# Weight pieces gated by the transfer four ahead of them instead of three, and the order planned anew with priorities varied unit by unit

## The chip, the cores and the metric

The kernel runs on one core of a Trainium2 chip. The metric is the device time of one execution in microseconds (us); less is better. The core's engines are TensorE (PE: matmuls, and PEld: its weight loads), VectorE (DVE), ScalarE (ACT), GpSimd (POOL) and SyncE (SP). SP computes nothing here: it issues most of the DMA transfers. Each engine works through its own instructions in the order in which the program emits them; an instruction waits for the semaphores of what it needs.

## The reference

Two stages in one kernel. First a gated linear attention over 4 x 8 heads, 768 positions and a head width of 48, then a two-layer MLP with an exact GELU over all 3072 tokens (model width 384, inner width 2048). All inputs are float32.

```python
f = 1 / (1 + exp(-f_logit))                       # [B, H, S, D] = 4, 8, 768, 48
for t in range(S):
    state = f[:, :, t, :, None] * state + einsum('bhd,bhe->bhde', k[:, :, t], v[:, :, t])
    y[:, :, t] = einsum('bhd,bhde->bhe', q[:, :, t], state)
x = y.transpose(0, 2, 1, 3).reshape(B * S, H * D)  # 3072 x 384
h = x @ w_in                                       # 3072 x 2048
g = 0.5 * h * (1 + erf(h / sqrt(2)))
out = g @ w_out                                    # 3072 x 384
```

## The kernel before

The attention is computed chunk by chunk: 24 chunks of 128 positions, six to a batch row. Two neighbouring chunks make a unit `u` (0 to 11), and the two chunks of a unit make one MLP group `g`. The state passes from chunk to chunk within a batch row and begins anew after six.

For a unit, four transfers bring `fl` (the logits), `kt`, `qt` and `vt`. `decays` has ScalarE compute an exponential and a logarithm (`E`, `L`, lines 466 and 469), TensorE the cumulative sum over the chunk (`C`, lines 482 to 492), ScalarE its exponentials both ways (`RG`, `GT`, lines 497 and 499), VectorE the scaled keys and queries in bf16 (`KP`, `QP`, line 512; two of them on POOL, by `GKP` and `GQP`), and POOL the bf16 copy `vb` of v (`VC`, line 517). `turn` transposes the scaled keys and queries: for the units in `KDMA` a DMA transpose on SP's queue (`KD`, line 533), else PE transposes into PSUM (`Tk`, `Tq`, line 545) and a copy out of it (`KQ`, line 551) by VectorE, or by ScalarE for the chunks in `HKQ`. The scores follow (`A`, lines 649 and 711), their mask on VectorE (line 558), the state (`S`, lines 672 and 733, with `carry` at lines 578 to 589) and the output `Y` (lines 626, 632, 685, 753). Units 0 to 4 (`PAIRS`) take two chunks at once, the rest one after the other.

`outputs` casts Y to bf16 (`YB`, line 602) and turns it for the MLP: for units in `XDMA` one DMA transpose on SP's queue (`XD`, line 606), else three PE transposes per chunk (`XT`, line 618) and a copy by VectorE (`X`, line 621). `ffn_group` then does F1 (line 789: eight steps of six matmuls over 256 tokens), the GELU on ScalarE (line 799), F2 (line 808: for each chunk four steps `r` of four matmuls, step `r` with weight piece `wout[r]`), the copy out of PSUM (lines 815 and 822) and the store on SP (line 824).

The MLP weights come in pieces, cast to bf16 by the transfer: w_in as `win[0]` (1024 columns) and `win[1]`, `win[2]` (512 each), w_out as `wout[0]` to `wout[3]`. POOL issues these (lines 433 and 436).

What sets the order of the work is a planner written into the kernel (`Plan`). Each step is an `Op` with an engine, an assumed duration, what it reads and writes, the buffers it takes, and a priority: 20 per unit for the attention, 1000 more for the MLP matmuls, so that these fill what attention leaves. `run` places the operations one after another on model clocks; among the ones that could start soonest the smaller priority goes first. Then the instructions are emitted in the order of their model starts. A random number within ±`SPREAD`, from the generator with `SEED`, is added to each priority, so that another seed gives another order. The model's numbers go into nothing but the order (and into the amount of filler: up to model time 30, gaps before PE steps are filled with matmuls of `junk`, line 847, whose results nobody reads).

The loads have a list of their own, `LOADS`, that fixes their order. A letter and a number name a piece: `f`, `k`, `q`, `v` the four inputs of a unit, `u` all four, `i` a piece of w_in, `o` a piece of w_out. A piece whose predecessor in the list was issued by the other engine waits for an earlier transfer (`gate`) to have landed:

```python
        if i and order[i - 1][0] != eng:
            back = 3 if eng == "pool" else 2
            for j in range(i - back, -1, -1):
                if order[j][0] != eng:
                    gate = order[j][1]
                    break
```

It looks back from the piece `back` places ahead of it for the nearest transfer of the other engine. By the list of before, i0 waits for v1, i1 for f2, o0 for nothing of its own (its predecessor is also POOL's), and q3 for o2. A wait holds up all that is behind it on the issuing engine: on SP later loads, stores and DMA transposes, on POOL its arithmetic.

Of the kernel before, what the change touches and what calls it, by code (L numbers as in the profile page):

```python
# [22 lines left out]

TURN = 0.1

SPREAD, SEED = (1.0, 78)

EAGER = 0.0

# [5 lines left out]
class Slots:  # L35


    def __init__(self, n, tiles=None):
        self.n, self.tiles = n, tiles
        self.who = [None] * n  # L40

    def new(self):
        return Buf(self)

    def free(self):

        out = []
        for i, b in enumerate(self.who):
            t = 0.0
            if b is not None:  # L50
                for u in b.users:
                    if u.end is None:
                        t = None
                        break
                    t = max(t, u.vis)
            if t is not None:
                out.append((t, i))
        return sorted(out)


class Buf:
# [14 lines left out]
class Plan:  # L76
# [30 lines left out]
    def run(self):  # L107
        free = dict.fromkeys(list(LAT), 0.7)
        free["DMA"] = 1.8
        rng = random.Random(SEED)  # L110
        for o in self.ops:
            if o.prio > -5:
                o.prio += rng.uniform(-SPREAD, SPREAD)
        act, switched, mode = None, 0.0, 0
        port = {"DVE": (0.0, 0.0), "POOL": (0.0, 0.0)}
        for o in self.ops:
            o.outs = []
        for o in self.ops:
            o.left = len(o.deps)
            for d in o.deps:  # L120
                d.outs.append(o)
        ready = [o for o in self.ops if not o.left]
        placed = []
        while ready:
            best = None
            for o in ready:
                t = free[o.eng]
                for d in o.deps:
                    v = d.end if d.eng == o.eng and (o.eng != "DMA" or d is o.chain) else d.vis + o.lag
                    t = v if v > t else t  # L130
                ok, taken = True, {}
                for b in o.bufs:
                    if b.slot is None:
                        v, k = b.slots.free(), taken.get(id(b.slots), 0)
                        if len(v) <= k:
                            ok = False
                            break
                        t = max(t, v[k][0])
                        taken[id(b.slots)] = k + 1
                if not ok:  # L140
                    continue
                x = t
                if o.table and act and o.table != act:
                    x = max(t, min(t + 2 * TABLE, max([d.vis for d in o.deps] + [switched]) + PATIENCE))
                pr = o.prio + (HOLD if o.held and act == "gelu" else 0.0)
                key = (int((x - (EAGER if o.eng == "PE" and o.prio < 900 else 0.0)) * 20 + 0.999), pr, o.seq)
                if best is None or key < best[0]:
                    best = (key, t, o)
            if best is None:
                raise RuntimeError("no operation can be placed: %s" % [o.name for o in ready[:20]])  # L150
            _, t, o = best
            d = o.dur
            if o.eng == "PE" and o.mode != mode:
                mode = o.mode
                d += TURN
            if o.port:
                other = port["POOL" if o.eng == "DVE" else "DVE"]
                d += SHARED * max(0.0, min(other[1], t + d) - max(other[0], t))
            if o.table and o.table != act:
                act, switched = o.table, t  # L160
                d += TABLE
            o.start, o.end = t, t + d
            o.vis = o.end + o.lat
            free[o.eng] = o.end
            for b in o.bufs:
                if b.slot is None:
                    b.slot = b.slots.free()[0][1]
                    b.slots.who[b.slot] = b
            ready.remove(o)
            placed.append(o)  # L170
            if o.port:
                port[o.eng] = (t, o.end)
            for n in o.outs:
                n.left -= 1
                if not n.left:
                    ready.append(n)
        if len(placed) != len(self.ops):
            raise RuntimeError("operations that wait for each other")
        placed.sort(key=lambda o: (o.start, o.seq))
        self.placed = placed  # L180
        return placed
# [14 lines left out]
WIN = [1024, 512, 512]  # L196
# [3 lines left out]
EA = []  # L200
SPLIT = []
HVC = []
HKQ = [0]
HYB = [1]
HX = []
GKP, GQP = ([2], [3])
GAM = []
ODVE = [0, 1, 2, 3, 4, 5, 6, 7, 8, 9, 10, 11, 12, 13, 14, 15, 16, 17, 18, 19, 20, 21, 22, 23]
XDMA = [3, 4, 5, 6, 7, 8, 9, 10, 11]
KDMA = [5, 6, 7, 8, 9, 10, 11]  # L210
AJ = [2, 3, 4, 5, 6, 7, 8, 9, 10, 11]
NGT = 4
WARM = 30.0
LOADS = ['f0', 'q0', 'k0', 'f1', 'v0', 'v1', 'k1', 'q1', 'i0', 'k2', 'f2', 'v2', 'q2', 'i1', 'i2', 'o0', 'o1', 'o2', 'o3', 'q3', 'f3', 'k3', 'v3', 'u4']
LOADS += [f"u{n}" for n in range(12) if f"u{n}" not in LOADS and f"c{2 * n}" not in LOADS and f"f{n}" not in LOADS]


@with_exitstack
def kernel(
# [134 lines left out]
    def load(eng, issue, wr, bufs, dur, name):  # L354
        i = len(order)
        gate = None
        if i and order[i - 1][0] != eng:
            back = 3 if eng == "pool" else 2
            for j in range(i - back, -1, -1):
                if order[j][0] != eng:  # L360
                    gate = order[j][1]
                    break
# [13 lines left out]
        if eng == "pool":  # L376
            if pools:
                gd.append(pools[-1])
            if i > 2 and order[i - 3][0] == "pool":
                gd.append(order[i - 3][1])  # L380
            k = P.add("POOL", 0.8, None, deps=gd, prio=-1000 + i, name="i" + name, lat=1.0)
            o = P.add("DMA", dur, lambda: None, wr=wr, bufs=bufs, prio=i, name=name, chain=prev, deps=[k])
            k.fn = lambda o=o: fn(o)
            pools.append(k)
        else:
            o = P.add("DMA", dur, None, wr=wr, bufs=bufs, prio=i, name=name, chain=prev, deps=gd)
            o.fn = lambda o=o: fn(o)
        if 7 <= i < 30 and o.lat < 1.8:
            o.lat = 1.8
        order.append((eng, o))  # L390

    def src(a, n):
# [9 lines left out]
    for what in LOADS:  # L402
        m = int(what[1:])
        if what[0] in "ucfkqv":
# [19 lines left out]
            else:  # L424
                for j in js:
                    for nm, a in names:
                        if what[0] not in ("u", "c", nm[0]):
# [1 line left out]
                        load("sp", lambda x=x, nm=nm, a=a, m=m, j=j: nc.sync.dma_start(  # L429
                            out=half(m, x[nm], j), in_=src(a, 2 * m + j)),  # L430
                            [(nm, 2 * m + j)], [x[nm]], 1.05, f"{nm}{m}.{j}")
        elif what[0] == "i":
            load("pool", lambda m=m: nc.gpsimd.dma_start(out=win[m], in_=win_src[:, :, wcol[m]:wcol[m] + WIN[m]]),
                 [f"win{m}"], [], {512: 1.97, 1024: 3.95}[WIN[m]] + (0.5 if order[-1][0] == "sp" else 0.0), what)
        elif what[0] == "o":
            load("pool", lambda m=m: nc.gpsimd.dma_start(out=wout[m], in_=wo_src[m]), [f"wout{m}"], [], 2.15, what)
# [450 lines left out]
```

## Time and profile before

| | |
|---|---|
| median of 4 runs | 185.45 us (184.78 to 187.68) |
| the profiled execution | 187.68 us, span 185.7 us, clock 0.991 |
| busy: PE, PEld, ACT, DVE, POOL | 173.9, 133.2, 121.4, 100.4, 53.2 us |
| F1 and F2 matmuls (lines 789, 808) | 69.1 and 67.6 us busy |
| filler matmuls (line 847) | 9.1 us busy |
| moved by DMA | 32.48 MB, 175 GB/s in the mean |

The span runs from the first to the last instruction; the execution's own time has some 2 us around it. In a line of the profile, the engine and the source line stand first, then the operation and its operands; "x18" is how many, and the bracket at the end is how long the engine sat idle before and what ended that. In tables by stretch, the columns are the length of the stretch, then busy time and number of instructions of PE, PEld, DVE, ACT, POOL, then the granted TensorE clock, the busy share of the DMA engines and GB/s. Waits are given as total, times and the longest, in us.

### The profile page before, as it was taken

What the parts mean: (1) busy time and instruction counts of PE and PEld (TensorE: products, weight loads), DVE (VectorE), ACT (ScalarE), POOL (GpSimd) and SP (SyncE); (2) the same over time, 40 slices, a digit from 0 to 9 for tenths busy, and PEclk for the clock granted to TensorE, in tenths of its full rate; (3) what the DMA queues carried; (4) which work ended last, traced back from release to release, by engine and by line L of the source; (5) the groups of instructions that cost most, each with busy time, mean ns of one, the idle gap of its engine ahead of it and who ended that gap; (6) DMA issues with size and microseconds to landing.
All of it is one profiled execution on the core that took longest, in us unless ns stands there. A gap on an engine that the chain in (4) does not pass through costs nothing.

```text
span 185.7 us, 4914 instructions
## 1 busy us (share of the span) xinstructions
PE 173.9 (94%) x1988; PEld 133.2 (72%) x1988; DVE 100.4 (54%) x190; ACT 121.4 (65%) x206; POOL 53.2 (29%) x118
## 2 busy tenths in 40 slices
PE   7897999999999969979999999999899999999992
PEld 2355779866787548967669976588689966797960
DVE  4377940079995898816374411696862717450120
ACT  2781198945769768968365799697589685272700
POOL 7359890005076231122124101424035114000000
PEclk9997899999999999999999999999999999999999
DMA  6999989999999799979899999599999933602112
GB/s 151 261 261 230 266 132 197 204 220 265 247 221 228 149 202 174 214 148 189 137 231 259 185 186 227 95 219 220 145 211 192 179 82 75 184 9 37 42 44 83
DMA packets 106421, 32.48 MB, mean 175 GB/s; under 512 B 101536, under 2 KB 105504, under 8 KB 106400
## 3 DMA queue, kind: packets, MB, share of 16 engines
q1 hardware_dynamic: 104480, 28.94, 75.2%
q0 software_dynamic: 1776, 3.15, 9.6%
q8 instruction: 15, 0.25, 0.6%
q10 hardware_dynamic: 144, 0.10, 0.2%
q14 instruction: 6, 0.05, 0.1%
HBM read 25.17 MB, written 4.72 MB: 161 GB/s over the span
## 4 chain that ended last, share of the span: by engine, by line
PE 68%; DMA 13%; DVE 5%; SPq 5%; ACT 4%; POOL 3%; issue 2%; DVEq 0%; POOLq 0%; ACTq 0%
PE ps L808 28%; PE ps L789 28%; DMA vt<-in_v_dram 8%; DMA xT<-yb 3%; SPq L421 3%; DVE sc L512 2%; DMA fl<-in_f_logit_dram 2%; PE ps L545 2%; PE ps L649 1%; SPq L429 1%; PE ps L482 1%; PE ps L685 1%; DVE kq L551 1%; POOL vb L517 1%; PE ps L672 1%
## 5 line engine op out<-in xcount | busy, mean ns | idle before, releaser
L799 ACT ACTIVATE gT<-ps 128x512 bf16<-128x512 f32 x96 | 58.0, 670 | 22.8 <-PE ps L789 21.5
L789 PE MATMUL ps<-xT,win 128*128 128x256 bf16 x576 | 69.1, 273 | 0.6 <-DMA xT<-yb 0.6
L808 PE MATMUL ps<-wout,gT 128*128 128x384 bf16 x384 | 67.6, 326 | 0.3 <-ACT gT L799 0.3
L789 PEld LDWEIGHTS <-win 128*128 128x128 bf16 x576 | 61.0, 114 | 2.2 <-issue 0.6
L808 PEld LDWEIGHTS <-gT 128*128 128x128 bf16 x384 | 36.2, 98 | 21.6 <-ACT gT L799 0.4
L822 DVE COPY osb<-ps 128x384 f32<-128x384 f32 x23 | 12.8, 555 | 30.8 <-PE ps L808 29.2
L517 POOL CAST vb<-vt 128x384 bf16<-128x384 f32 x24 | 12.1, 516 | 51.0 <-DMA vt<-in_v_dram 51.0
L512 DVE TENSOR_TENSOR sc<-kt,rg 128x384 bf16<-128x384 f32 x23 | 14.0, 613 | 22.1 <-ACT rg L497 17.1
L584 POOL TENSOR_TENSOR tn<-rr,gl 128x384 f32<-128x384 f32 x16 | 14.2, 889 | 34.1 <-DVE rr L582 28.4
L558 DVE TENSOR_TENSOR am<-ps,mask 128x512 bf16<-128x512 f32 x28 | 17.4, 684 | 12.0 <-PE ps L649 11.4
L589 POOL CAST sb<-tn 48x192 bf16<-48x192 f32 x40 | 15.2, 381 | 17.0 <-DVE tn L578 8.6
L853 ACT ACT_TABLE_LOAD x15 | 19.2, 1283 | 0.3
L497 ACT ACTIVATE rg<-ps 128x384 f32<-128x384 f32 x24 | 11.9, 499 | 11.4 <-PE ps L484 5.8
L466 ACT ACTIVATE fl<-fl 128x768 f32<-128x768 f32 x12 | 10.2, 847 | 13.5 <-DMA fl<-in_f_logit_dram 13.3
L512 DVE TENSOR_TENSOR sc<-qt,gt 128x384 bf16<-128x384 f32 x23 | 15.1, 667 | 0.9 <-ACT gt L499 0.9
L602 DVE CAST yb<-ps 128x384 bf16<-128x384 f32 x23 | 12.4, 554 | 4.5 <-PE ps L685 3.0
L499 ACT ACTIVATE gt<-ps 128x384 f32<-128x384 f32 x24 | 11.7, 500 | 3.3 <-PE ps L484 3.3
L558 DVE TENSOR_TENSOR am<-ps,maskp 128x512 bf16<-128x512 f32 x20 | 12.4, 683 | 1.7 <-PE ps L711 1.6
L582 DVE TENSOR_TENSOR rr<-ps,tn 128x384 f32<-128x384 f32 x16 | 8.8, 551 | 5.8 <-PE ps L672 3.0
L847 PE MATMUL ps<-junk 128*128 128x512 bf16 (+2 forms) x28 | 9.1, 464 | 1.4 <-POOL junk L839 1.3
L469 ACT ACTIVATE lf<-fl 128x768 bf16<-128x768 f32 x12 | 10.1, 843 | 0.4
L545 PE MATMUL ps<-ident,sc 128*128 128x128 bf16 x80 | 7.6, 234 | 2.1 <-DVE sc L512 1.1
(65 smaller groups left out, 120.1 us busy)
## 6 DMA issues: line engine op xcount, KB each, us to landing
out_dram<-osb SPq DMA_DIRECT2D x23, 192.0 KB, 2.4
fl<-in_f_logit_dram SPq DMA_DIRECT2D x14, 192.0 KB, 4.2
kt<-in_k_dram SPq DMA_DIRECT2D x14, 192.0 KB, 3.8
qt<-in_q_dram SPq DMA_DIRECT2D x14, 192.0 KB, 3.6
vt<-in_v_dram SPq DMA_DIRECT2D x14, 192.0 KB, 3.8
fl<-in_f_logit_dram SPq DMA_DIRECT2D x5, 384.0 KB, 6.0
qt<-in_q_dram SPq DMA_DIRECT2D x5, 384.0 KB, 4.8
kt<-in_k_dram SPq DMA_DIRECT2D x5, 384.0 KB, 6.2
```

Source lines behind the costliest of these rows:

```text
L497: P.add("ACT", 0.40, lambda g=gps[j], rg=rg: nc.scalar.activation(rg.t(), g.t()[:, 0:HD], AF.Exp, scale=-1.0), rd=[("g", n)], wr=[("rg", n ...
L512: P.add("POOL" if pl else "DVE", 0.80 if pl else 0.475, lambda w=w, a=a, b=b, y=y, j=j, pl=pl: (nc.gpsimd if pl else nc.vector).tensor_tensor(
L517: P.add("ACT" if hv else "POOL", 0.40 if hv else 0.47, lambda y=y, j=j, hv=hv: (nc.scalar.copy if hv else nc.gpsimd.tensor_copy)(y["vb"].t ...
L558: P.add("POOL" if pl else "DVE", 1.15 if pl else 0.61, lambda hh=hh, pl=pl: (nc.gpsimd if pl else nc.vector).tensor_tensor(ams[hh].t(), ap ...
L584: P.add("POOL", 0.83, lambda: nc.gpsimd.tensor_tensor(tn.t(), rr.t(), glb(), ALU.mult), rd=[("rr", n), ("gl", n)], wr=[("tn", n)], bufs=[r ...
L589: P.add("POOL", 0.36, lambda hh=hh: nc.gpsimd.tensor_copy(sb.t()[64 * hh:64 * hh + D, :, D * hh:D * hh + D], tn.t()[64 * hh:64 * hh + D, : ...
L602: P.add("ACT" if help_ else "DVE", 0.40 if help_ else 0.475, lambda: copier(help_)(yb.t()[:, i, :], yp.t()[:, 0:HD]), rd=[("yp", n)], wr=[ ...
L789: nc.tensor.matmul(hps.t()[:, i * tok:(i + 1) * tok].rearrange("a (s t) -> a s t", s=s), col(fo)[:, kk, :], xT.t()[:, :, kk, :], start=(kk ...
L799: nc.scalar.activation(to, fr, AF.Gelu)
L808: nc.tensor.matmul(op.t()[:, 0:d_model], gT.t()[:, fo, s_ * C:(s_ + 1) * C], wout[fo // 4][:, fo % 4, :], start=(fo == 0), stop=(fo == FO ...
L822: P.add("DVE" if od else "ACT", 0.475 if od else 0.40, lambda op=op, osb=osb, od=od: copier(not od)(osb.t(), op.t()[:, 0:d_model]), rd=[(" ...
L853: nc.scalar.preload_act_table_set({"exp": "natural_log_exp_and_others", "gelu": "gelu_and_others"}[o.table])
```

## The change

- A weight piece is gated by the nearest transfer of the other engine at least four places ahead of it, instead of three. SP's gates stay at two.
- `LOADS`: v0 moves ahead of q0 and f1, k0 ahead of q0; o3 goes ahead of o2 and f3 between them; k3 stands ahead of q3. With the new list i0 waits for f1 (now fifth), i1 for k2, f3 for o1, o2 for q2, k3 for o3. The name `i3` in the list issues nothing, since there are three pieces.
- `XDMA` loses units 3 and 4: their output is turned by PE and copied by VectorE.
- `HKQ` gains chunk 2: ScalarE copies its transposed keys and queries instead of VectorE.
- The seed is another, and each unit may add a random number of its own: `SEEDS` has one entry per unit, and its rest after division by four chooses the width.
- The model has three other numbers (the delay of POOL's issue and of gated loads on SP, the landing of i0), and free slots are remembered within the planner. No instruction comes from these lines but through the order.

```diff
-SPREAD, SEED = (1.0, 78)
+SPREAD, SEED = (1.0, 97)
+
+SEEDS = [0, 3, 358, 3531, 1454, 1223, 983, 3849, 2582, 1403, 2107, 2867]
...
         rng = random.Random(SEED)
+        own = [random.Random(x) for x in SEEDS]
         for o in self.ops:
             if o.prio > -5:
+                k = min(max(int(o.prio % 1000) // 20, 0), len(SEEDS) - 1)
                 o.prio += rng.uniform(-SPREAD, SPREAD)
+                if SEEDS[k]:
+                    w = (0.5, 1.0, 3.0, 8.0)[SEEDS[k] % 4]
+                    o.prio += own[k].uniform(-w, w)
...
-HKQ = [0]
+HKQ = [0, 2]
...
-XDMA = [3, 4, 5, 6, 7, 8, 9, 10, 11]
+XDMA = [5, 6, 7, 8, 9, 10, 11]
...
-LOADS = ['f0', 'q0', 'k0', 'f1', 'v0', 'v1', 'k1', 'q1', 'i0', 'k2', 'f2', 'v2', 'q2', 'i1', 'i2', 'o0', 'o1', 'o2', 'o3', 'q3', 'f3', 'k3', 'v3', 'u4']
+LOADS = ['f0', 'k0', 'v0', 'q0', 'f1', 'v1', 'k1', 'q1', 'i0', 'k2', 'f2', 'v2', 'q2', 'i1', 'i2', 'i3', 'o0', 'o1', 'o3', 'f3', 'o2', 'k3', 'q3', 'v3', 'u4']
...
-            back = 3 if eng == "pool" else 2
+            back = 4 if eng == "pool" else 2
...
-            k = P.add("POOL", 0.8, None, deps=gd, prio=-1000 + i, name="i" + name, lat=1.0)
+            k = P.add("POOL", 0.8, None, deps=gd, prio=-1000 + i, name="i" + name, lat=1.3)
...
-            o = P.add("DMA", dur, None, wr=wr, bufs=bufs, prio=i, name=name, chain=prev, deps=gd)
+            o = P.add("DMA", dur, None, wr=wr, bufs=bufs, prio=i, name=name, chain=prev, deps=gd, lag=1.5 if gd else 0.0)
...
-            o.lat = 1.8
+            o.lat = 2.0 if name == "i0" else 1.8
...
-        elif what[0] == "i":
+        elif what[0] == "i" and m < len(WIN):
```

More of the change, by code (lines that the diff above doesn't have):

```diff
@@ L40, in __init__ @@
         self.who = [None] * n
+        self.memo = None
     def new(self):
@@ L45, in free @@
     def free(self):
+        if self.memo is not None:
+            return self.memo
         out = []
@@ L57, in free @@
                 out.append((t, i))
-        return sorted(out)
+        self.memo = sorted(out)
+        return self.memo
 class Buf:
@@ L168, in run @@
                     b.slots.who[b.slot] = b
+                b.slots.memo = None
             ready.remove(o)
```

## The prediction

> **What bounds the kernel now.** I read the page first: busy time, then the slices.
>
> ```profile
> PE 173.9 (94%) x1988; PEld 133.2 (72%) x1988; DVE 100.4 (54%) x190; ACT 121.4 (65%) x206; POOL 53.2 (29%) x118
> ...
> PE   7897999999999969979999999999899999999992
> ...
> L808 PE MATMUL ps<-wout,gT 128*128 128x384 bf16 x384 | 67.6, 326 | 0.3 <-ACT gT L799 0.3
> ```
>
> TensorE (PE) is busy 94% of 185.7 us, so no other engine can hand over much. But its busy time includes filler: the multiplications of `junk` (L847). Their busy time by stretch (columns: us, PE, PEld, POOL, clock, DMA share, GB/s):
>
> ```profile
> 0.00:22.00 22.00, 8.27 (x25) 2.77 (x25) 0.52 (x1) 0.92 1.11 232
> 22.00:40.00 18.00, 0.81 (x3) 0.22 (x3) 0.00 (x0) 1.00 0.99 186
> ```
>
> So real work is 173.9 - 9.1 = 164.8 us, and 20.9 us of the span is filler or idleness. Busy time by 5 us stretches places the idleness: 3.9 in the first 20, some 3.6 in the tail behind the last matmul (ends at 182.1), and 4.3 in the middle. TensorE's waits name most of the middle:
>
> ```profile
> PE ps L482 <- ACT lf L469: 1.5, 1, 1.5
> ...
> PE ps L672 <- POOL vb L517: 1.3, 1, 1.3
> ...
> PE ps L789 <- DMA xT<-yb: 0.6, 1, 0.6
> ```
>
> The chain of waits in order of time shows what is behind the first two: a late f load (issued 64.47, landed 67.84; E and L on ScalarE; the cumulative sum starts at 69.69) and a late v load:
>
> ```profile
> 74.68 0.70 DVE am L558
> 75.39 0.48 SPq L606
> 75.92 4.98 DMA vt<-in_v_dram
> 80.94 0.08 issue
> 81.02 0.51 POOL vb L517
> 81.58 0.33 PE ps L672 x4
> ```
>
> That v load stood in SP's queue behind `XD` (L606), which waited for VectorE. In the head, timelines of POOL and PE set the first MLP matmul:
>
> ```profile
> 12.38 0.94 POOL L433 DMA_DIRECT2D win<-in_moe_w_in_dram  x1 [0.80 <-DMA vt<-in_v_dram]
> 22.92 1.58 POOL L433 DMA_DIRECT2D win<-in_moe_w_in_dram  x2 [0.20 <-issue]
> ```
>
> ```profile
> 19.48 0.97 PE L847 MATMUL ps<-junk 128*128 128x512 bf16 x3
> 20.54 0.88 PE L711 MATMUL ps<-kq 64*64 64x128 bf16 x32
> 21.35 0.50 PE L847 MATMUL ps<-junk 128*128 128x512 bf16 x2
> 21.69 2.13 PE L789 MATMUL ps<-xT,win 128*128 128x256 bf16 x18
> ```
>
> The first weight piece is issued at 12.38 and took 9.1 us to land (the line's own answer): 21.48, just ahead of the first F1 at 21.69. Its input `xT` was ready at 18.76 (last copy 18.41 + 0.35). Filler bridges the difference.
>
> SP's waits show the other long gate, q3 behind o2:
>
> ```profile
> SPq L421 <- DMA wout<-in_moe_w_out_dram: 17.4, 1, 17.4
> ```
>
> **What the Trainium skill says.** "DMA: Bandwidth & Descriptors", section "Issuing engines are not separate DMA queues": transfers of all issuers share 16 engines and interleave. The trace agrees: a 384 KB load took 3.9 us alone at 36.7, 6.2 among others at 5.9, and 10.3 beside a weight piece at 15.0. Same page, "Anatomy of one DMA": the issuing sequencer does a transfer's semaphore wait, not the DMA engines; here SP stood 17.4 us. "TensorE: Matmul & The Clock Gate", "Step-by-step: what each phase is for": matmuls stay in program order; at 81.58 F1 work stood behind one `vb`. The same page's part 1 says that idleness lowers the clock; the grant was 0.66 in 15 to 20 us, where PE was busy 4.18 of 5, and 1.00 from 20 on.
>
> **The change, part by part.**
>
> *Gate of i0, new head order.* Landings (issue plus time to landing): f0 4.54, q0 6.06, k0 7.57, f1 9.08, v0 10.6, v1 12.08. The old gate is v1, sixth; the new one is f1, now fifth, so 10.6: i0 is issued about 1.5 earlier (POOL is free, since v0, now third, has its casts done by 8.6). At the same 9.1 us it lands at 20.0. F1 can then start 1.5 earlier, and the fillers at 19.48 and 21.35 have 0.97 + 0.50 = 1.47 to give. It shares the engines with k1 and q1 for 1.5 us longer; at half rate each is 0.7 late. They landed at 13.57 and 15.05 and were used at 14.23 and 15.87: slack 0.66 and 0.82, so hidden, barely; without that cover unit 1 moves by up to 0.7. q0 and f1 each land 1.5 later: the unit-0 scores, at 10.89, move by some 0.5 and have 2.7 of slack at 18.76. Range 0 to -1.5; I take -1.2.
>
> *Gate of i1.* From f2 (landed 22.57) to k2 (17.44): i1, i2 and the o pieces, issued back to back from 22.92 to 27.6, may go up to 5 us earlier. The 0.67 us of filler at 26.91 can go. f2, v2, q2 (22.6 to 25.3) pay for it; ScalarE already waited 5.5 for f2, but PE had 11 us of pure MLP after 27.58. Range 0 to -0.7; I take -0.4.
>
> *o pieces and f3.* f3 waits for o1 (26.0 + 8.0 = 34.0) and stands ahead of q3, instead of behind q3, which waited for o2 (36.7): at least 2.7 earlier. The DMA was nearly empty for 1.6 us there (92, 15, 54, 92 GB/s per 0.4 us), which the new order fills. Behind that gate in SP's queue stand k3, q3, v3, u4 and all later loads, so the benefit is for the late loads after 55. I credit half of the 1.5 stall at 69.69: -0.7 (0 to -1.5). Against it, o2 is now the last weight; F2 began at 35.27 while o2 and o3 landed at 36.7 and 38.6, which leaves a reserve of r = 0, 1 work for four chunks, 8 x 0.65 = 5.2 us. Cost 0, and up to 1.5 if that reserve isn't queued first.
>
> *XDMA without 3 and 4.* PE gets 4 x 3 transposes. The chain prices three at 0.17: +0.7 us, with nothing to hide it. VectorE gets 4 copies of 0.357 = 1.4 us, beside PE unless it is full. SP loses two transposes (1.67 and 1.25 us of issue) and their waits for `yb`; the v load behind the second can go at 74.5 instead of 75.92, lands 1.4 earlier and closes the 1.28 stall: -1.3 (0 if another step holds SP).
>
> *HKQ with 2.* VectorE loses 0.684; ScalarE gets 0.99, where it sat idle 5.5 us (17.2 to 22.6): 0, at most +0.3 when F1 waits on that.
>
> *Seeds, lags.* The order of all engines is new; no row prices that. Below, all of the remaining middle idleness, 4.3 - 2.8 = -1.5; above, as much new as there was, +4.3; one switch of ScalarE's table (1283 ns) more or less lies inside this. I take +0.4. The planner's memo and its lag numbers issue nothing.
>
> Sum: -1.2 - 0.4 - 0.7 + 0.7 - 1.3 + 0.4 = -2.5. The profiled execution took 187.68 with its 185.7 span (2.0 around it), the longest of four; it would become 185.2. The median, 185.45, becomes 183.0.
>
> **The rivals.**
>
> *The transfers bind anyway.* From 5 to 37 us the DMA share is 0.86 to 1.29 of full in every stretch. An earlier i0 only permutes: f2, v2, q2 or the last weight come later by as much, and the head's 1.6 comes back as waits at F2 or unit 2. Then -1.6 goes, and with half of the middle gain: 185.45 + 0.7 - 1.0 + 0.4 = 185.5. For it: F2 starts within 3.4 us of the last weight. Against it: the empty 1.6 us.
>
> *VectorE takes over (slower).* In 40 to 55 VectorE is busy 4.7 to 4.9 of 5, and here in the third stretch of the middle (same columns, DVE third):
>
> ```profile
> 65.00:70.00 5.00, 3.53 (x58) 2.26 (x56) 4.85 (x10) 3.08 (x8) 1.76 (x3) 1.00 1.03 202
> ```
>
> Each new transpose waits in PE's queue for a cast (0.557), and F1 for a copy (0.357): exposed in full, 4 x 0.91 = 3.7. With 0.7 of transposes, nothing gained in the middle and 1.2 in the head: 185.45 + 3.7 + 0.7 - 1.2 = 188.6. It decides against the change once more than 2.4 of those 3.7 is exposed (185.45 + 2.4 + 0.7 - 1.2 = 187.3). Against it: PE has MLP work of other groups to put between.
>
> *The change doesn't do it:* i0 is planned behind other POOL work, and gate and order give nothing but +0.7: 186.1; counted with the first rival.
>
> **How the numbers follow.** Forecast 0.50, its own range 180.5 to 184.2 (all gains and -1.5, to no gain of i1 and f3); first rival 0.30, 184.2 to 186.8; second 0.20, above it. A measurement of this kernel tells about 1% (1.9 us) from no change. Faster than 183.6 takes 0.49: most of the forecast and a little more; within 1% takes 0.32, slower 0.19. The range leaves out some 0.07 below 180.5 and 0.13 above 187.6.
>
> **What would show it.** i0's issue near 10.9 and its landing near 20; first F1 at 20 to 20.5; `junk` below 8 us; f3's issue at 34 or earlier, no empty DMA at 37; 30 matmuls at L618's counterpart and 7 transposes of `xT` on SP; no wait of L672's counterpart for `vb` over 0.5. Wrong if the middle's idleness exceeds 4.3, if PE waits for `yb` or `xT` of units 3 and 4, or F2 waits for o2.

## The result

The changed kernel takes 184.47 us in the median of 40 runs (184.11 to 185.44); the kernel before, beside it, 185.57 us in 61 runs (184.59 to 187.92). The ratio is 0.9945, 95% interval 0.9932 to 0.9957: faster by 0.55%, 1.0 to 1.1 us, less than half of the 2.5 us forecast, and within the 1% that counted as no change. Its profiled execution took 184.72 us, with a span of 182.7 us.

The page of the changed kernel, lines as shown of before (busy time, PE's slices, F2; the changed file's lines stand 12 further down than the old one's, so L808 is now L820, L789 is L801, L847 is L859, L618 is L630):

```profile
PE 173.4 (95%) x2006; PEld 133.0 (73%) x2006; DVE 99.7 (55%) x193; ACT 122.2 (67%) x207; POOL 55.3 (30%) x118
...
PE   7787999999999998999999999999999999999991
...
L820 PE MATMUL ps<-wout,gT 128*128 128x384 bf16 x384 | 69.0, 326 | 0.0
```

PE is no less busy than before, and the holes that the slices of before showed in the middle are gone. The filler alone, by stretch (columns as before: us, PE, PEld, POOL, clock, DMA share, GB/s):

```profile
0.00:22.00 22.00, 9.48 (x31) 3.15 (x31) 0.52 (x1) 1.00 1.10 232
22.00:40.00 18.00, 0.81 (x3) 0.29 (x3) 0.00 (x0) 1.00 1.06 206
```

Filler grew from 28 to 34 matmuls and from 9.1 to 10.3 us; the forecast had it fall below 8. The view of PE's waits from 28 us on lists two (total, times, longest, in us):

```profile
PE ps L630 <- DVE yb L614: 0.5, 1, 0.5
PE ps L801 <- ACT gT L811: 0.3, 1, 0.3
```

The waits for `lf`, `vb` and `xT` that the prediction showed of before are absent. POOL's and PE's timelines in the head:

```profile
10.84 0.94 POOL L445 DMA_DIRECT2D win<-in_moe_w_in_dram  x1 [1.80 <-DMA fl<-in_f_logit_dram]
...
21.50 1.58 POOL L445 DMA_DIRECT2D win<-in_moe_w_in_dram  x2
```

```profile
18.79 0.59 PE L859 MATMUL ps<-junk 128*128 128x512 bf16 x2
...
20.75 2.13 PE L801 MATMUL ps<-xT,win 128*128 128x256 bf16 x18
...
26.16 0.81 PE L859 MATMUL ps<-junk 128*128 128x512 bf16 x3 [0.19 <-ACT gT L811]
26.80 3.44 PE L801 MATMUL ps<-xT,win 128*128 128x256 bf16 x30
```

i0 is issued at 10.84 and lands 9.7 later, at 20.54; the first F1 is at 20.75 (21.69 before). But F1 is broken up by attention and filler until its third stretch, at 26.80 (27.42 before); from there on PE runs without a break, and I call that the steady F1. The chain of waits says why:

```profile
11.70 10.61 DMA fl<-in_f_logit_dram
...
22.33 0.85 ACT fl L478
...
24.07 1.28 ACT L865
...
25.37 0.75 ACT gT L811
...
26.16 0.81 PE ps L859 x3
...
26.97 7.86 PE ps L801 x72
```

The head ends on f2's transfer, unit 2's exponential and logarithm on ScalarE, the load of the GELU table, the first GELU, and a filler that waited for the PSUM which that GELU frees. The first weight piece isn't in it.

SP's wait for o1 ended with f3's issue at 34.55 (37.21 before). In 65 to 70 us VectorE is full, 5.00 of 5 us, and PE is busy 4.88 beside it (before: 4.85 and 3.53).

### The profile page after: what moved, and what is told of

Its sections match the earlier page's. It is cut to its first block, busy times and chain, and to the rows that moved or that the text cites. A ratio compares the mean times of both kernels' runs of the same rounds, so it can differ in the third digit from the quotient of the medians.

```text
span 182.7 us, 4932 instructions
## 1 busy us (share of the span) xinstructions
PE 173.4 (95%) x2006; PEld 133.0 (73%) x2006; DVE 99.7 (55%) x193; ACT 122.2 (67%) x207; POOL 55.3 (30%) x118
## 4 chain that ended last, share of the span: by engine, by line
PE 73%; DMA 8%; SPq 8%; DVE 3%; ACT 3%; issue 2%; DVEq 0%
PE ps L820 32%; PE ps L801 29%; DMA fl<-in_f_logit_dram 8%; SPq L433 6%; PE ps L661 2%; SPq L441 2%; PE ps L697 1%; ACT L865 1%; PE ps L557 1%; PE ps L494 1%; DVE am L570 1%; PE ps L638 1%; ACT fl L478 1%; DVE sc L524 1%; ACT gT L811 1%
## 5 line engine op out<-in xcount | busy, mean ns | idle before, releaser
L801 PE MATMUL ps<-xT,win 128*128 128x256 bf16 x576 | 69.0, 273 | 0.3 <-ACT gT L811 0.3
L820 PE MATMUL ps<-wout,gT 128*128 128x384 bf16 x384 | 69.0, 326 | 0.0
L801 PEld LDWEIGHTS <-win 128*128 128x128 bf16 x576 | 61.4, 114 | 2.5 <-issue 0.4
L820 PEld LDWEIGHTS <-gT 128*128 128x128 bf16 x384 | 35.9, 98 | 20.3
L529 POOL CAST vb<-vt 128x384 bf16<-128x384 f32 x24 | 13.2, 563 | 53.3 <-DMA vt<-in_v_dram 53.2
L524 DVE TENSOR_TENSOR sc<-qt,gt 128x384 bf16<-128x384 f32 x23 | 13.7, 611 | 17.0 <-ACT gt L511 16.5
L865 ACT ACT_TABLE_LOAD x15 | 19.2, 1283 | 0.3
L859 PE MATMUL ps<-junk 128*128 128x512 bf16 (+3 forms) x34 | 10.3, 435 | 1.5 <-POOL junk L851 1.3
L557 PE MATMUL ps<-ident,sc 128*128 128x128 bf16 x80 | 6.5, 220 | 1.3 <-POOL sc L524 0.8
```

Of the source, the lines that this page charges most:

```text
L524: P.add("POOL" if pl else "DVE", 0.80 if pl else 0.475, lambda w=w, a=a, b=b, y=y, j=j, pl=pl: (nc.gpsimd if pl else nc.vector).tensor_tensor(
L529: P.add("ACT" if hv else "POOL", 0.40 if hv else 0.47, lambda y=y, j=j, hv=hv: (nc.scalar.copy if hv else nc.gpsimd.tensor_copy)(y["vb"].t ...
L801: nc.tensor.matmul(hps.t()[:, i * tok:(i + 1) * tok].rearrange("a (s t) -> a s t", s=s), col(fo)[:, kk, :], xT.t()[:, :, kk, :], start=(kk ...
L820: nc.tensor.matmul(op.t()[:, 0:d_model], gT.t()[:, fo, s_ * C:(s_ + 1) * C], wout[fo // 4][:, fo % 4, :], start=(fo == 0), stop=(fo == FO ...
L865: nc.scalar.preload_act_table_set({"exp": "natural_log_exp_and_others", "gelu": "gelu_and_others"}[o.table])
```

## The experiments

Ratios are to the kernel before, run on the same chip, with 95% intervals. Unless a text says that the order was planned anew, all other instructions kept the order of their kernel.

### The kernel before a second time

No edit.

> The kernel before, unchanged, profiled a second time. Theory M (the profiled execution of before was an unusual one: it lasted 187.68 us against a median of 185.57): a second execution takes 184.6 to 186 us, and its two long stalls in the middle (1.5 us for an f load at 69.7, 1.3 us for a v load at 81.6) are together under 1.5 us instead of 2.8. Rival N (the stalls belong to the order): both come back within 0.4 us each, with an idle middle of about 4.3 us.

This execution took 184.91 us with a span of 182.9, against 187.68 for the one that the prediction was made from. All of PE's waits from 28 us on:

```profile
PE ps L482 <- DVE am L558: 0.8, 1, 0.8
PE ps L545 <- DVE sc L512: 0.5, 1, 0.5
PE ps L808 <- ACT gT L799: 0.3, 1, 0.3
```

The 1.5 for a late f load, the 1.3 for a late v load and the 0.6 for a transpose, on which 2.0 us of the forecast rested, aren't there. Stalls of this kind, for late loads in the middle, go with long executions: the profile of 187.68 has them, and so do those of the old order, below, with one load moved or gated otherwise (186.72 and 187.09) or with less filler (186.11), in varying places; this one of 184.91 and the one with the gate moved (185.09) have none. If an execution of the median length, 185.57, is otherwise like this one, it can have only some 0.7 of them (185.57 - 184.91). The steady F1 of this profile:

```profile
27.57 8.02 PE L789 MATMUL ps<-xT,win 128*128 128x256 bf16 x72
```

Against it the changed kernel's comes 0.77 earlier (26.80), PE is busy 0.93 longer from there on (151.06 against 150.13, 12 transposes among it), and 0.36 of its idleness there is gone (4.84 against 5.20): the two spans, 182.9 and 182.7, are nearly the same.

### The gate, in both orders

In the kernel before, POOL's gates four back, list and order kept: the planner still counts with the old gate, and the instruction waits for `held`.

```diff
+        held = gate
+        if gate is not None and eng == "pool":
+            held = next(order[j][1] for j in range(i - 4, -1, -1) if order[j][0] != eng)
...
-            if gate is not None:
+            if held is not None:
...
-                    ins.ins, gate.inst.ins.name,
+                    ins.ins, held.inst.ins.name,
```

> The order of before kept instruction by instruction, only the waits of the weight pieces moved to the transfer four ahead (i0 on v0 instead of v1, i1 on k2 instead of f2). Theory G (the gate of i0 sets the head, as predicted): i0 is issued some 0.8 us earlier (behind the two casts of v0), the first F1 and with it the steady F1 come as much earlier, ratio 0.995. Theory F (f2's landing sets the head, over E, L, ScalarE's table load and the first GELU): the steady F1 does not move by more than 0.2 us, ratio 0.998 to 1.002, or above 1 if f2 lands later.

185.61 us, ratio 1.0001 (0.9968 to 1.0034): nothing. i0 was issued at 11.43 instead of 12.29 and took 10.3 us instead of 9.5, so that it landed at the same 21.7 to 21.8, and the first F1 waited 0.6 for it. The earlier issue bought no earlier landing. The next weight piece, i1, was issued at 21.95 instead of 23.11, and that bought nothing that the time shows either.

In the changed kernel, POOL's gates three back, by the same lines with another number:

```diff
+            held = next(order[j][1] for j in range(i - 3, -1, -1) if order[j][0] != eng)
```

> The order of after kept, only the waits of the weight pieces moved back to the transfer three ahead (i0 on v1, i1 on f2). Theory G: i0 is issued 1.4 us later, the time rises by 1.2 to 1.5 us, ratio to before 1.001 to 1.003 instead of 0.9945. Theory F: the steady F1 depends on f2, which lands no later (or earlier) with i0 later: ratio 0.993 to 0.997, and the first F1 alone moves.

188.08 us, ratio 1.0116 (1.0069 to 1.0164): 3.2 us slower than the changed kernel, by the two ratios. i0 was issued at 12.27, 1.43 later than at 10.84, and landed 9.2 later. That isn't where the time went. POOL in this run:

```profile
12.27 0.94 POOL L448 DMA_DIRECT2D win<-in_moe_w_in_dram  x1 [3.17 <-DMA vt<-in_v_dram]
...
17.25 0.98 POOL L527 TENSOR_TENSOR sc<-kt,rg 128x384 bf16<-128x384 f32 x1
18.20 0.99 POOL L527 TENSOR_TENSOR sc<-qt,gt 128x384 bf16<-128x384 f32 x1
```

and PE:

```profile
18.29 0.61 PE L560 MATMUL ps<-ident,sc 128*128 128x128 bf16 x4 [2.59 <-POOL sc L527]
```

POOL stood still at the gate with the state's casts and the scaled keys of chunk 2 behind it. The keys were done 1.7 us later (18.23 instead of 16.51), PE waited 2.59 us for them (0.79 in the changed kernel), and its transposes of them began 1.72 later (18.29 instead of 16.57). The steady F1 came at 30.28, 3.48 later, and the rest of that is not waiting. From these transposes to the first F1 PE has the same instructions in both runs; they took 4.18 us in the changed kernel (16.57 to 20.75), at a granted clock of 1.00, and 6.26 here without an idle moment (18.29 to 24.55), at 0.60 in 16 to 20 us and 0.55 in 20 to 24. Pieces of it, the changed kernel first:

```profile
16.57 0.40 PE L557 MATMUL ps<-ident,sc 128*128 128x128 bf16 x4 [0.79 <-POOL sc L524]
...
17.69 0.83 PE L557 MATMUL ps<-ident,sc 128*128 128x128 bf16 x12
18.36 1.03 PE L859 MATMUL ps<-junk 128*128 128x512 bf16 x4
...
20.75 2.13 PE L801 MATMUL ps<-xT,win 128*128 128x256 bf16 x18
```

```profile
20.20 1.49 PE L560 MATMUL ps<-ident,sc 128*128 128x128 bf16 x12
21.48 1.91 PE L862 MATMUL ps<-junk 128*128 128x512 bf16 x4
...
24.55 2.13 PE L804 MATMUL ps<-xT,win 128*128 128x256 bf16 x18
```

All six executions of this run have a mean granted clock of 0.979 to 0.991, all of the changed kernel 0.995 or more. So the late gate costs 3 us in the new order in two parts: 1.7 us for arithmetic that stands behind the issue, and some 2 us of a lowered clock after it (0.3 is made up again ahead of the steady F1). That the wait brought the clock down is not tested apart from it. The second gate that moved, i1's, is not what held PE: i1 went out 2.75 later (24.25), and none of PE's waits is for a weight piece. What a gate costs is what queues behind it, and what follows from that.

### What ends the head

Two edits, alone and together: f2 issued ahead of k2 in the changed kernel (i1 still waits for k2), and filler up to an earlier model time, 24 instead of 30, in both kernels (18 in one run):

```diff
+        held = gate
+        if name == "i1":
+            held = order[10][1]
...
+    a, b = [next(o for o in P.ops if o.name == x) for x in ("kt2", "fl2")]
+    a.fn, b.fn = b.fn, a.fn
```

```diff
-WARM = 30.0
+WARM = 24.0
```

> The order of after, with f2 issued ahead of k2 (the two change places in SP's queue; i1 still waits for the ninth transfer of SP). Theory F: f2 lands 1.5 us or more earlier, E and L of unit 2 and the table load follow, the first GELU starts up to 1.5 us earlier, the filler of 0.8 us at 26.2 and the wait behind it go, and the steady F1 starts 0.6 to 0.8 us earlier: ratio to before 0.990 to 0.992. Theory G: nothing on the path moves, ratio 0.994 to 0.996.

> After, with filler only up to model time 24: the three filler matmuls at 26.2 go. Theory F (the steady F1 waits for a PSUM buffer that the first GELU frees, and that for f2): the filler went where PE would have waited 0.2 us anyway; the steady F1 starts at 26.1 to 26.4 instead of 26.8, ratio to before 0.991 to 0.994. Rival (PE waits for ScalarE right away once the filler is gone): ratio as after, 0.994 to 0.995.

> The order of after, f2 ahead of k2 as in the run with f2 first, and filler only up to model time 24, which takes out the three filler matmuls ahead of the steady F1. Theory (with f2 early the filler itself is what holds the steady F1): it starts 0.5 to 0.65 us earlier, at 25.8 to 25.9, ratio to before 0.989 to 0.992. Rival (a later wait gives it back): ratio 0.993 to 0.995.

> As the kernel with f2 ahead of k2 and filler up to model time 24, with filler only up to 18: seven more junk matmuls fewer, behind unit 2's and unit 1's transposes. If filler still holds the first F1 there: 183.5 (a ratio of 0.988), the steady F1 some 0.5 earlier than 25.95. If first F1 is held by the weight piece's landing and the GELUs, as the waits there say: 184.1, with the filler's time turned into idleness.

> The kernel before with filler only up to model time 24 in place of 30: the three junk matmuls at 26.92 go (0.65 us of path). If they held its steady F1, as in the changed kernel: 185.0 (a ratio of 0.997). If the second weight piece or the GELU holds it there: 185.5.

| | us | ratio (95%) | steady F1 |
|---|---|---|---|
| changed | 184.47 | 0.9945 (0.9932 to 0.9957) | 26.80 |
| f2 ahead of k2 | 184.41 | 0.9935 (0.9911 to 0.9959) | 26.43 |
| filler to 24 | 184.05 | 0.9920 (0.9890 to 0.9950) | 26.29 |
| both | 184.09 | 0.9910 (0.9876 to 0.9944) | 25.95 |
| f2 ahead, filler to 18 | 184.01 | 0.9880 (0.9826 to 0.9934) | 26.18 |
| before, filler to 24 | 185.11 | 0.9951 (0.9914 to 0.9988) | 26.92 |

With f2 first it lands at 20.9 instead of 22.3, and the first GELU starts at 23.95 instead of 25.37. The steady F1 gains only 0.37 of these 1.42, since the three fillers ahead of it (25.78 to 26.43) are fixed in PE's order. With both it begins straight behind the cumulative sum:

```profile
25.74 0.34 PE L507 MATMUL ps<-negp,lf 128*128 128x2 bf16 x8
25.95 4.32 PE L804 MATMUL ps<-xT,win 128*128 128x256 bf16 x38
```

So both bounds are real, and a third lies close behind: with the filler taken away down to 18, PE waits for the weight piece itself (0.69), and nothing more is gained. The versions with less filler beat the changed kernel by 0.4 us in their medians, though their intervals overlap its own. The old kernel gains by the same edit too: its fillers at 26.92 held it, and its steady F1 comes 0.65 earlier without them. By ratio this one line is worth to the old kernel about what the whole change is (0.9951 and 0.9945), with a wide interval, and on a chip on which the kernel before took 186.17; against the median of all its executions, 185.57, it is 0.46 us. The last row but one is from that chip too.

### The transposes of units 3 and 4

The changed kernel with these two units turned on SP's queue, as before; their PE transposes and copies issue nothing, and the DMA transpose takes the place of the second copy:

```diff
-        P.add("PE", 0.17, xmm, rd=[("yb", n), "ident"], wr=[("xp", n)], bufs=[yb, xp, xT], prio=pr + PRI["X"], opens=xp, name=f"XT{n}")
+        xd = u in (3, 4)
+        P.add("PE", 0.17, (lambda: None) if xd else xmm, rd=[("yb", n), "ident"], wr=[("xp", n)], bufs=[yb, xp, xT], prio=pr + PRI["X"], opens=xp, name=f"XT{n}")
...
-        P.add("ACT" if hx else "DVE", 0.39 if hx else 0.27, lambda: copier(hx)(xT.t()[:, j], xpv()),
+        P.add("ACT" if hx else "DVE", 0.39 if hx else 0.27, (lambda: None if not i else nc.sync.dma_start_transpose(
+            xT.t().rearrange("a s i t -> a (s i) t"), yb.t().rearrange("p s e -> p (s e)"))) if xd else lambda: copier(hx)(xT.t()[:, j], xpv()),
```

> The order of after kept, but units 3 and 4 turn their output with one DMA transpose each on SP (issued where after has the second copy), as before, in place of 12 PE transposes and 4 VectorE copies. Theory Q (SP's queue: the two transposes stood in front of loads, and taking them away is what makes the time of after low and steady): the time rises by 0.5 us or more, to 185.0 to 186, and scatters like before's (over 2 us from lowest to highest, against 1.3). Rival P (the transposes on PE only cost, as the sum had them at +0.7): the time falls by 0.4 to 0.8 us, to 183.7 to 184.1, with the scatter of after.

187.32 us, ratio 1.0098 (1.0060 to 1.0137): 2.8 us slower than the changed kernel. SP's queue in this run, and PE's waits:

```profile
72.30 1.05 SPq L838 DMA_DIRECT2D out_dram<-osb  x2
73.45 0.39 SPq L441 DMA_DIRECT2D fl<-in_f_logit_dram  x1
73.94 1.32 SPq L634 DMA_TRANSPOSE xT<-yb  x1
```

```profile
PE ps L803 <- ACT gT L813: 3.2, 3, 1.3
```

The f load that the changed kernel issues at 71.87 goes at 73.45, and the next one, behind the second transpose, at 77.60 instead of 74.94 (changed kernel first):

```profile
74.94 0.74 SPq L441 DMA_DIRECT2D fl<-in_f_logit_dram  x1
```

```profile
77.60 0.95 SPq L441 DMA_DIRECT2D fl<-in_f_logit_dram  x1
```

For the latter ScalarE waited 2.3 here (0.4 there), the GELUs stood behind that, and F1 behind their PSUM. VectorE, spared four copies, brought nothing. The run prices the transposes at this place in SP's queue; a planner might have put them elsewhere.

The other way round, the kernel before with these units turned by PE, planned anew with the same seed and the same random number for every other operation, so that the order differs only from unit 3 on:

```diff
-            if o.prio > -5:
+            if o.prio > -5 and o.name not in ("XT6", "X6", "XT7", "X7", "XT8", "X8", "XT9", "X9"):
...
-XDMA = [3, 4, 5, 6, 7, 8, 9, 10, 11]
+XDMA = [5, 6, 7, 8, 9, 10, 11]
```

> The kernel before with one part of the change alone: units 3 and 4 turned by PE (12 transposes, 4 VectorE copies), planned with the same seed and the same random offsets for all other operations, so that the order is the old one up to unit 3. Theory Q (the DMA transposes of these units in SP's queue are what makes loads late and the old kernel's executions differ from one another): the median falls to about 184.6 (a ratio of 0.995), the spread of the executions shrinks to that of the new kernel, about 1.3 us, and no cumulative sum or vb wait over 0.5 us is in the middle. Rival S (the order drawn by the seeds is what counts): 185.5 or more, with 0.7 of transposes added, and the executions spread over 3 us as before.

188.87 us, ratio 1.0172 (1.0137 to 1.0208): the same part that saves 2.8 us in the new order comes with 3.2 us more in the old one, drawn anew from unit 3 on. Two stretches in which PE had no idleness in the second profile of before now read (columns: us, PE, PEld, DVE, ACT, POOL, clock, DMA share, GB/s):

```profile
70.00:80.00 10.00, 8.96 (x139) 7.58 (x137) 8.65 (x18) 8.20 (x16) 2.89 (x6) 1.00 0.94 168
140.00:160.00 20.00, 18.59 (x189) 15.03 (x187) 10.97 (x20) 18.87 (x34) 5.61 (x10) 1.00 0.45 98
```

2.45 us of new idleness lie there. In 70 to 80 PE waited 0.6 for a cast of `yb` ahead of the new transposes (L618); at 155 the state's matmul (L672) waited 1.2 for scaled keys, in a stretch where ScalarE worked 18.87 of 20 us (12.22 in before). ScalarE changed tables more often:

```profile
L853 ACT ACT_TABLE_LOAD x17 | 21.8, 1283 | 0.3
```

Before and the changed kernel both have 15. The head of this run, in the same order as before, also began its steady F1 0.56 later than the second profile of before, at a granted clock of 0.50 in 16 to 20 us. My theory of this run was refuted. Its executions lie close together (188.44 to 189.11, while those of before beside it ran from 184.78 to 188.27), as it had said, but at 3 us more. The kernel with the list added, below, also has these transposes on PE; of its four executions three lie within 0.9 us and one 3.1 above them, too few to say. So what makes the old kernel's executions differ isn't settled. Its measured executions show one thing more: the 51 with a mean granted clock of 0.991 have a median of 185.15, and the 30 with 1.000 one of 186.24. Where the clock was lower, with the gate three back, the same matmuls took longer, so the two groups must differ in something else as well; no run looked for it.

### Single loads behind the gates and the transposes

In the kernel before, q3 gated by o1 instead of o2; and the v load that stood behind unit 4's transpose put ahead of it:

```diff
+        held = order[16][1] if name == "qt3" else gate
```

```diff
+    i = next(i for i, o in enumerate(P.placed) if o.name == "XD9")
+    j = next(j for j in range(i + 1, len(P.placed)) if P.placed[j].eng == "DMA")
+    P.placed.insert(i, P.placed.pop(j))
```

> The order of before kept, only q3 waits for o1 instead of o2, so that SP is released at about 34.5 instead of 36.9, as in after. Theory S (the late loads of the middle, which come and go between executions of before, hang on this release): the time falls by 0.5 to 0.8 us (ratio 0.996 to 0.997) and scatters less, no execution above 186.3. Rival (the loads of the middle hang on buffers coming free and on the wait for the transfer eight ahead on SP, not on this gate): ratio 0.999 to 1.001, scatter as before's.

> The order of before kept, only the output transpose of unit 4 and the v load of unit 6 behind it change places in SP's queue. Theory Q (that v load, held up by the wait of the transpose, is what PE waits for in some executions of before): the wait for the copy of v near 81 is gone, the median falls by 0.4 to 0.7 us (ratio 0.996 to 0.998) and the slowest executions, above 186.5, go. Rival (the late load is chance of the DMA engines and comes whatever stands ahead): ratio 0.999 to 1.002, scatter as before.

185.96 us, ratio 1.0014 (0.9985 to 1.0043), and 185.64 us, ratio 1.0000 (0.9973 to 1.0026). In the first, SP came free at 35.23 instead of 36.98, and the middle still had its waits (vb 1.23, xT 0.51). In the second the wait for `vb` is gone, and others stand in its place (lf 1.06, kq 0.74, gT 0.43). Neither is what holds the old kernel up.

### ScalarE's copy

The changed kernel with chunk 2's transposed keys and queries copied by VectorE:

```diff
-            P.add("ACT" if help_ else "DVE", 0.86 if help_ else 0.61, lambda tpv=tpv, j=j, help_=help_: copier(help_)(
+            P.add("ACT" if help_ else "DVE", 0.86 if help_ else 0.61, lambda tpv=tpv, j=j, help_=help_ and n != 2: copier(help_)(
```

> The order of after kept, only the copy of chunk 2's transposed keys and queries goes back from ScalarE to VectorE, where it stands behind the other copy. The prediction's step (0, at most +0.3 for the change): ratio to before within 0.001 of 0.9945. Rival (VectorE is full in the head: two copies in a row of 0.68 us delay the scores of unit 1): the scores move from 19.6 to 19.9 or later, ratio 0.996 to 0.997.

184.41 us, ratio 0.9945 (0.9924 to 0.9966), the changed kernel's own: worth nothing, as forecast.

### The seeds and the parts, planned anew

Five more kernels were planned anew. Two are the changed kernel without the offsets per unit, with its own seed and with before's:

```diff
-SEEDS = [0, 3, 358, 3531, 1454, 1223, 983, 3849, 2582, 1403, 2107, 2867]
+SEEDS = [0] * 12
```

```diff
-SPREAD, SEED = (1.0, 97)
+SPREAD, SEED = (1.0, 78)
```

> After with all entries of SEEDS zero: gates, lists, XDMA, HKQ and seed 97 as in after, but planned without the numbers of single units. Theory O (the choice of the order carries the gain): slower than after by 1 us or more, ratio to before above 1.000. Theory E (the other edits carry it): ratio 0.993 to 0.997.

> After with SEEDS zero and the seed of before, 78: a second order with the same other edits. Theory O: another time again, over 0.5 us from the run with seed 97, and not below after. Theory E: ratio 0.993 to 0.997 like the other.

Three are the kernel before: with the new `LOADS` and the gate four back; with these and units 3 and 4 turned by PE as above; and with the seed 97 alone:

```diff
-LOADS = ['f0', 'q0', 'k0', 'f1', 'v0', 'v1', 'k1', 'q1', 'i0', 'k2', 'f2', 'v2', 'q2', 'i1', 'i2', 'o0', 'o1', 'o2', 'o3', 'q3', 'f3', 'k3', 'v3', 'u4']
+LOADS = ['f0', 'k0', 'v0', 'q0', 'f1', 'v1', 'k1', 'q1', 'i0', 'k2', 'f2', 'v2', 'q2', 'i1', 'i2', 'i3', 'o0', 'o1', 'o3', 'f3', 'o2', 'k3', 'q3', 'v3', 'u4']
...
-            back = 3 if eng == "pool" else 2
+            back = 4 if eng == "pool" else 2
```

> The kernel before with the new list of loads and the gate four back, its own seed, order planned anew: the second part alone. If list and gate carry the gain: about 184.7 (0.996), with the steady F1 0.7 earlier than before's 27.5. If the gate is only as good as the order of POOL's queue that goes with it: anywhere from 185.5 up, with POOL waiting in front of arithmetic.

> The kernel before with both: the new list and gate, and units 3 and 4 turned by PE; the old seed without unit offsets. If the parts add up and the seeds only vary the outcome by some tenths: the changed kernel's 184.5. If the seeds carry it: unlike 184.5 by more than 1 us, and the difference is found in the middle as waits of PE.

> The kernel before with the seed 97 and nothing else. If a seed alone moves the time by as much as the whole change: outside 184.9 to 186.2. If one seed is as good as another for the old settings: within that, a ratio of 0.997 to 1.003.

| planned anew | us | ratio (95%) | table loads | PE busy | steady F1 |
|---|---|---|---|---|---|
| before (two profiles) | 185.57 | 1 | 15, 15 | 173.9, 171.7 | 27.42, 27.57 |
| changed | 184.47 | 0.9945 (0.9932 to 0.9957) | 15 | 173.4 | 26.80 |
| changed, no unit offsets | 185.07 | 0.9970 (0.9949 to 0.9991) | 15 | 173.4 | 26.66 |
| changed, no unit offsets, seed 78 | 188.68 | 1.0157 (1.0109 to 1.0205) | 17 | 174.8 | 26.99 |
| before, units 3 and 4 on PE | 188.87 | 1.0172 (1.0137 to 1.0208) | 17 | 176.0 | 28.13 |
| before, list and gate | 193.41 | 1.0410 (1.0339 to 1.0481) | 23 | 177.7 | 28.52 |
| before, list, gate and units 3, 4 | 191.98 | 1.0329 (1.0276 to 1.0382) | 15 | 175.3 | 27.31 |
| before, seed 97 | 187.11 | 1.0062 (1.0029 to 1.0096) | 15 | 173.8 | 28.21 |

No part of the change made the old kernel faster. The list with its gate, alone, cost 7.7 us, though i0 was issued at 10.83 as in the changed kernel and landed by 20.9: there the first F1 stood in PE's order behind eight fillers and the scores of line 711 (22.25), and later ScalarE changed tables 8 times more:

```profile
L853 ACT ACT_TABLE_LOAD x23 | 29.5, 1283 | 0.4
```

That is 10.3 us of ScalarE (29.5 - 19.2). It isn't the whole story: adding the transposes brings the table loads back to 15 and the time only to 191.98, with 3.5 us of PE's idleness in 60 to 90 us (30 less 26.53; 1.1 in the second profile of before). 2.2 of these are waits of F1 for GELUs; why the GELUs were late wasn't taken apart further. Without the offsets per unit the changed kernel has lost 0.6 of its 1.1 us, by the medians (185.07; the two intervals overlap a little). What these runs show is that the same settings under another seed lie 3.6 us apart (185.07 and 188.68), more than three times the whole effect of the change.

## Why the prediction was wrong

**The two credits in the middle were priced from a stall that isn't the kernel's own.** This is the step that failed: -0.7 for f3 and the o pieces, and -1.3 for the v load behind the transpose. Both were read off waits of the profiled execution, 187.68 us, 1.6% longer than the shortest of its four, and subtracted from the median, 185.45, as if each execution had them. The second profile has neither. On the median there was, by the estimate above, some 0.7 to take, not 2.0. f3 was issued at 34.55, half a microsecond past the 34 foretold, and this bought nothing that a run shows (the earlier q3: 1.0014). The closed wait for `vb`, tried by itself, gave 1.0000. The prediction did state that its execution was the longest of four, and then carried its waits over all the same.

**The head: direction right, size halved, and the wrong last wait.** -1.2 and -0.4 were forecast, -0.77 came against the second profile of before. i0's issue at 10.84 is the one foretold (10.9), the landing at 20.54 and the first F1 at 20.75 are 0.3 to 0.5 later than foretold. But the sum ended at the first F1, and the head ends 6 us later, where f2's transfer, a table load, a GELU and three fillers meet. The filler ahead of it did not go, it grew, since its amount comes from the model's gaps and not from those of the chip. That the gate's gain is not the transfer's was also missed: in the old order an issue 0.86 earlier moved the landing by 0.1.

**The price of a wait on POOL.** The sentence that POOL is free for an earlier issue was right; that everything behind that issue also moves was left out. In the new order, the gate three back costs 3 us (1.0116): 1.7 us of late keys and some 2 us of the lowered clock that came with them.

**Transposes.** +0.7 for PE was right in kind: PE is busy 0.93 longer from the steady F1 on. That SP's queue gains more than PE loses is borne out in the new order (2.8 us net); in the old kernel, drawn anew, the same part came with a loss of 3.2, so the gain is no property of the part alone.

**ScalarE's copy, 0:** measured 0. **Seeds, +0.4 within -1.5 to +4.3:** the range was about right: seed 97 made the old kernel 0.6% slower, and two draws of the changed one lie 3.6 us apart. Of the 1.1 us gained, 0.6 goes with the offsets per unit, as far as the medians tell.

**The rivals.** VectorE did not take over: PE was busy 4.88 us of the 5 in which VectorE was full, and its one wait for `yb` from 28 us on was 0.5. That wait, at 72.56, is for unit 4, one of the prediction's own signs of being wrong; it is small. The first rival, that the transfers bind anyway, gave 185.5 and named f2 among those that pay; f2 does end the head, and in the old order the earlier issue only permuted the landings. But the last weight and F2 never met. The measured 184.47 lies in the lower end of the range that the prediction gave this rival, 184.2 to 186.8. The ends of the forecast's own range don't follow from its terms: without the gains of i1 and f3 the sum is 184.05, not 184.2, and 180.5 has f3 at -0.7, not at the -1.5 that its range allows.

**How the parts come to -1.1.** From the second profile of before to the profile of the changed kernel it is -0.2: -0.77 in the head, +0.93 of PE work, -0.36 of idleness. Further -0.66 is the distance of before's median from that execution, and -0.25 that of the changed kernel's profile from its own median. These two, 0.9 of the 1.1 us, only say where the two profiled executions lie among the others; they are not traced to a part. The old kernel's executions scatter more (184.59 to 187.92 against 184.11 to 185.44), and late loads that differ from one execution to the next are what their profiles show. That the changed kernel lacks the scatter is measured; why, among order, list and transposes, stays open.

## What to carry to other kernels

A stall that is read off one execution is worth what the median has of it: look at a second profile of the same kernel before a wait is credited, above all when the profiled execution is the longest. A gate is priced by what queues behind it on the issuing engine as well as by when its transfer lands. Where a planner draws the order, a part of a change has no price of its own: redraw the order a few times, with and without it, before a difference of one per cent is put down to the part.

## What was not expected of the hardware

- A 768 KB weight piece that was issued 0.86 us earlier among loads landed 0.1 earlier (9.5 us to landing became 10.3).
- In 16 to 20 us the granted clock was 0.57 in the first profile of before and 1.00 in the second, with the same instructions; the steady F1 began at 27.42 with the dip and 27.57 without. The slower matmuls filled what were waits in the other execution: PE was busy 3.78 of these 4 us with the dip and 2.81 without, so the stretch with more idleness was the one with the full clock. With the gate three back in the changed kernel, where the dip went on to 24 us and PE had no waits left to fill, it cost some 2 us.
- ScalarE needed 15, 17 or 23 table loads (1283 ns each) for the same work, by its order alone.
